# Attention with two feed-forward layers on one core: twenty conversion steps in the attention, fp32 centroid strips for every pair

## The chip, the cores and the metric

The kernel runs on one core of one Trainium2 chip. The metric is the time of one execution in device microseconds (us); lower is better. Of three executions shown for the kernel before, the median is 794.51 us (793.96 to 795.6).

## The reference

Clustered attention comes first, then two feed-forward layers. q, k and v have two batches, 8 heads, 768 rows and 64 columns; there are 16 centroids for each head. A row of q attends to the rows of k that have the same nearest centroid.

```python
q_assign = np.argmax(np.einsum('bhsd,hcd->bhsc', q_n, c_n), axis=-1)
k_assign = np.argmax(np.einsum('bhsd,hcd->bhsc', k_n, c_n), axis=-1)
mask = q_assign[:, :, :, None] == k_assign[:, :, None, :]
scores = np.where(mask, scale * q @ k.T, -1e9); attn = softmax(scores)
x = (attn @ v) reshaped to 1536 x 512
h = x @ w_in;  x = (h * cos(h)) @ w_out          # layer 0
h = x @ w_in2; x = g(h) @ w_out2                 # layer 1, g = a quadratic blend to a ReLU
```

All inputs are float32 except the four weight matrices (512 x 2048 and 2048 x 512), which come as float64.

## The kernel before

**Number format.** A large matmul takes each operand as a high and a low fp32r part (`hi`, the rounded value; `lo`, the rest). The scores use stacked tiles `st` that hold both parts, the layers use three matmuls for each product (`mm3`, L748 to L751).

**Weights.** The float64 weights come in 32 chunks of 1 MB (`wraw`, one buffer; `issue_chunk`, L130, on SP's queue). `convert_chunk` (L138) turns one chunk to fp32 with integer operations: Abs on ACT (L145), clamp, shift and two ORs on DVE (L147 to L155), hi on POOL (L161) with the issue of the next chunk behind it, lo on DVE (L164). The yields make six steps of it, and `pump(1)` does one step. In the attention, `run_slot` pumps at slots 69, 77, ... 189 (L686), 16 steps. In the layers, each of the four parts of `hidden` and `output` pumps one step; `weight` pumps what is missing. Two chunks make one weight tile: chunks 0 and 1 make `w_0`, which exists during the attention, chunks 2 and 3 make `w_1`, which exists only after it (L708).

**Attention.** A pair is two heads of one batch; there are eight. A pair has four units of six slots, so the attention has 192 slots. In a slot, `run_slot` (L664) emits for PE the transposes of the probabilities (L569), a score matmul pair for the unit ahead (L517, L520; eight slots ahead), and products with v (L594, L599, L600). DVE takes the row maximum (L526) and the low parts (L584), ACT the exponent (L535, in even slots) and the copies of the transposes (L572, L577, one in each slot). Slots before 18 and after 179 are ordered by readiness when the program is built; from 18 to 179 PE, ACT, DVE and POOL keep the order of the program (L694), SP does not.

**Preparation of a pair** (`prep_pair`, L294) runs a step in each slot, from slot -8 for pair 1 and 24(i-1)-16 for pair i. q and k are transposed (L349), copied from PSUM on ACT (L358), split to `th` and `tl`, and stacked by DMAs on SP's queue (L335; for pair 0 partly copied on POOL, L332). Then come the dot products with the centroids, and the argmax on DVE and POOL. Its one-hot rows are transposed (L434, L491) and written to `st`, for pair 0 by ACT and DVE (L446, L448), for the others by eight DMAs (L312) behind the next v load (L232), which waits until POOL has read the tile before it (L481, L482). PSUM gives three buffers for all of the transposes (`ps_t`).

- Pairs 0 and 1 (`NDVE`): DVE makes the low part (L316), and 24 matmuls of 64 columns (L408, L409) with the centroids as high and low part (`cn`) make the dots, which DVE then adds up (L377).
- Pairs 2 to 7: POOL splits (L321, L322), four fp32 matmuls of 32 rows each (strips, L389) with `cn32` make the dots, ACT copies them (L393), three transposes bring them back (L398).

**The start** has no other work for PE, so `run_idle` (L220) issues matmuls on zeros there; `NIDLE` gives their counts.

**The sums of a unit**: `inverse` (L541) adds the constant on POOL, five slots later DVE takes the reciprocal (L548), then POOL spreads it (L555).

Of the kernel before, what the change touches and what calls it, by code (L numbers as in the profile page):

```python
# [1 line left out]

# [6 lines left out]
F32 = mybir.dt.float32  # L9
# [9 lines left out]
P = 128  # L19
# [6 lines left out]
CHUNK = 6  # L26
P_BUFS = 6
NF = 2
NDVE = 2
NIDLE = (9, 3, 5, 7, 6)  # L30
# [3 lines left out]
def attention_moe_moe(  # L34
# [66 lines left out]
    cn = cpool.tile([P, NPAIR, 2, 2, C], F32R, name="cn")  # L101
# [36 lines left out]
    def convert_chunk(n):  # L138
# [4 lines left out]
        x = w0pool.tile([P, 2, 512], F32, tag="wx", bufs=1, name=f"wx{n}")  # L143
# [4 lines left out]
        yield  # L148
# [13 lines left out]
        issue_chunk(n + 1)  # L162
# [33 lines left out]
    with ExitStack() as actx:  # L196
# [44 lines left out]
        def centroid_setup(ct):  # L241
# [21 lines left out]
            nc.vector.memset(cn.bitcast(F32), 0.0)  # L263
# [3 lines left out]
        def centroid_parts(cd):  # L267
# [12 lines left out]
        def centroid_sum():  # L280

            for r in range(2):
                rows = slice(r * D, (r + 1) * D)
                nc.gpsimd.tensor_tensor(
                    cn32[rows, :, r], cn[rows, :, 0, r].bitcast(F32),
                    cn[rows, :, 1, r].bitcast(F32), ALU.add)
# [7 lines left out]
        def prep_pair(i):  # L294
# [19 lines left out]
            def qk_parts(s, cols, t32, pt, sc):  # L314
                if i < NDVE:
# [28 lines left out]
            for s in range(2):  # L344
                sc = D ** -0.5 if s == 0 else 1.0
                for hf in range(2):
# [6 lines left out]
                    if i < NDVE:  # L353
                        t32 = th[:, s, cols]
                    else:
                        t32 = ap.tile([P, HS], F32, tag="t32", bufs=4, name=f"t32_{i}_{s}_{hf}")
# [19 lines left out]
            def sum_dots(s, pd):  # L376
                nc.vector.tensor_reduce(  # L377
                    dotv[s].rearrange("p j h c -> p j (h c)"),
                    pd.rearrange("p j t h c -> p j (h c) t"), AX.X, ALU.add)

            rhs = cn[:, hp].rearrange("p t h c -> p (t h c)")
            pd32 = None
            if i >= NDVE:

                dt = ps_t.tile([P, HS], F32, tag="t", name=f"dt{i}")
                for hf in range(2):
                    for s in range(2):
                        g = (hf * 2 + s) * 2 * C
                        nc.tensor.matmul(  # L389
                            dt[g:g + 2 * C], cn32[:, hp].rearrange("p h c -> p (h c)"),  # L390
                            t32s[(s, hf)], start=True, stop=True, tile_position=(0, g))
# [9 lines left out]
            for s in range(2 if i < NDVE else 0):  # L401
                pd = ps_t.tile([P, NJ, 2, 2, C], F32, tag="t", name=f"pd{i}_{s}")
                for j in range(NJ):
                    cols = slice(j * P, (j + 1) * P)
                    o = pd[:, j if i == 0 else j % HJ * 2 + j // HJ].rearrange(
                        "p t h c -> p (t h c)")
                    with tc.issue_after(ins(tr)) if i == 0 else ExitStack():
                        nc.tensor.matmul(o, th[:, s, cols], rhs, start=True, stop=False)  # L408
# [430 lines left out]
```

## Time and profile before

| what | value |
|---|---|
| median of 3 executions | 794.51 us |
| the profiled execution, its own time | 794.65 us |
| its span, first to last instruction | 792.8 us |
| PE, DVE, ACT, POOL busy | 98%, 75%, 51%, 35% |
| mean granted clock of TensorE | 0.996 |

The span is the time between the first and the last instruction in the trace; 1.85 us of the execution lie outside it. PE's busy share says how long a matmul was under way. The granted clock is 1.00 at 2.4 GHz and 0.50 at 1.2 GHz.

### The profile page before, as it was taken

The page shows a single profiled execution, that of the slowest core. Times are in us where ns is not written, and L with a number is a line of the kernel's source. Part 1 is how long each engine was busy: PE and PEld are TensorE (multiplying, and loading weights), DVE is VectorE, ACT ScalarE, POOL GpSimd, SP SyncE. Part 2 cuts the span into 40 slices and gives each one's busy share as a digit, 9 for nine tenths or more (in the row PEclk, how much of TensorE's full clock was granted, in tenths as well). Part 3 has the DMA queues.
Part 4 walks back from the last instruction along what each step waited for, and adds up shares of the span by engine and source line. Part 5 has one row for each costly group of instructions (what it writes and reads, how often), then busy time and mean ns, then how long its engine had stood idle before and what let it go on. Part 6 is the DMA issues. An engine that isn't in the chain of part 4 may idle for free.

```text
span 792.8 us, 10973 instructions
## 1 busy us (share of the span) xinstructions
PE 779.4 (98%) x3963; PEld 635.9 (80%) x3964; DVE 596.7 (75%) x881; ACT 400.7 (51%) x768; POOL 275.8 (35%) x428
## 2 busy tenths in 40 slices
PE   8999999999999989999999999999999999999998
PEld 5777877878787868888888888888888888888886
DVE  6867877977989587778787878888878888655552
ACT  3788888888898555453334344322434323222220
POOL 4257567578545431221122212342131122111110
PEclk9999999999999999999999999999999999999999
DMA  7764754663420013222131121311121221000012
GB/s 167 172 153 113 176 130 105 144 175 94 106 79 29 26 53 107 79 81 107 54 98 62 58 101 54 107 54 53 58 103 54 90 71 53 1 1 0 22 46 93
DMA packets 48565, 65.94 MB, mean 83 GB/s; under 512 B 28032, under 2 KB 33024, under 8 KB 48512
## 3 DMA queue, kind: packets, MB, share of 16 engines
q1 hardware_dynamic: 48368, 65.22, 28.7%
q8 instruction: 31, 0.51, 0.3%
q14 instruction: 22, 0.18, 0.1%
q10 hardware_dynamic: 144, 0.03, 0.0%
HBM read 43.02 MB, written 3.15 MB: 58 GB/s over the span
## 4 chain that ended last, share of the span: by engine, by line
PE 88%; DVE 5%; ACT 4%; issue 1%; POOL 1%; SPq 1%; DMA 0%; ACTq 0%; POOLq 0%
PE y L751 11%; PE y L749 11%; PE y L750 11%; PE h L751 10%; PE h L749 10%; PE h L750 10%; PE pt L569 8%; PE s L517 4%; PE s L520 3%; PE o L594 2%; PE o L600 2%; PE o L599 2%; ACT p L535 1%; PE ptq L349 1%; DVE nm L526 1%
## 5 line engine op out<-in xcount | busy, mean ns | idle before, releaser
L711 POOL TENSOR_SCALAR gh<-g 128x512 fp32r<-128x512 f32 x96 | 70.9, 739 | 289.2 <-DVE g L742 163.8
L749 PE MATMUL h<-xh,w 128*128 128x512 f32 x384 | 149.5, 389 | 0.0
L751 PE MATMUL h<-xh,w 128*128 128x512 f32 x384 | 149.4, 389 | 0.0
L750 PE MATMUL h<-xl,w 128*128 128x512 f32 x384 | 149.4, 389 | 0.0
L526 DVE TENSOR_REDUCE nm<-s 128x1 f32<-128x768 f32 x96 | 91.4, 953 | 33.3 <-PE s L520 32.6
L569 PE MATMUL pt<-ident,p 128*128 128x128 f32 x576 | 98.2, 279 | 2.6 <-DVE plo L584 1.7
L738 ACT ACTIVATE p<-h,ones 128x512 f32<-128x512 f32 x48 | 33.0, 688 | 132.5 <-DVE m L737 132.1
L569 PEld LDWEIGHTS pt<-ident,p 128*128 128x128 f32 x576 | 68.3, 140 | 31.4 <-DVE nm L526 9.0
L535 ACT ACTIVATE p<-s,nm 128x768 f32<-128x768 f32 x96 | 86.4, 900 | 6.6 <-DVE nm L526 5.7
L715 DVE TENSOR_TENSOR gl<-g,gh 128x512 fp32r<-128x512 f32 x96 | 71.1, 741 | 20.8 <-POOL gh L711 15.0
L750 PEld LDWEIGHTS h<-xl,w 128*128 128x128 f32 x384 | 72.1, 188 | 15.0
L751 PEld LDWEIGHTS h<-xh,w 128*128 128x128 f32 x384 | 72.1, 188 | 15.0
L749 PEld LDWEIGHTS h<-xh,w 128*128 128x128 f32 x384 | 72.1, 188 | 14.9
L517 PE MATMUL s<-st,st 128*128 128x384 f32 x192 | 80.5, 419 | 1.5 <-ACT p L535 1.4
L145 ACT ACTIVATE wx<-wraw 128x1024 f32<-128x1024 f32 x32 | 36.4, 1138 | 88.0 <-DMA wraw<-in_moe_w_in_dram 32.7
L584 DVE TENSOR_TENSOR plo<-pt,phi 128x384 fp32r<-128x384 f32 x128 | 67.9, 549 | 14.1 <-ACT phi L577 13.8
L751 PE MATMUL y<-gh,w 128*128 128x512 f32 x192 | 75.6, 394 | 2.7 <-DVE w L164 2.7
L749 PE MATMUL y<-gh,w 128*128 128x512 f32 x192 | 75.3, 392 | 0.0
L750 PE MATMUL y<-gl,w 128*128 128x512 f32 x192 | 75.2, 392 | 0.0
L751 PE MATMUL y<-w,gl 128*128 128x512 f32 x192 | 74.7, 389 | 0.0
L749 PE MATMUL y<-w,gh 128*128 128x512 f32 x192 | 74.7, 389 | 0.0
L750 PE MATMUL y<-w,gh 128*128 128x512 f32 x192 | 74.7, 389 | 0.0
(132 smaller groups left out, 1530.0 us busy)
## 6 DMA issues: line engine op xcount, KB each, us to landing
wraw<-in_moe_w_in_dram SPq DMA_DIRECT2D x16, 1024.0 KB, 5.1
wraw<-in_moe_w_out_dram SPq DMA_DIRECT2D x16, 1024.0 KB, 4.7
st<-t SPq DMA_DIRECT2D x24, 192.0 KB, 4.2
st<-th SPq DMA_DIRECT2D x9, 384.0 KB, 4.0
st<-tl SPq DMA_DIRECT2D x18, 192.0 KB, 4.0
st<-th SPq DMA_DIRECT2D x18, 192.0 KB, 3.9
nat<-in_q_dram SPq DMA_DIRECT2D x8, 384.0 KB, 3.9
nat<-in_k_dram SPq DMA_DIRECT2D x8, 384.0 KB, 5.1
```

Of the source, the lines that this page charges most:

```text
L145: nc.scalar.activation(x, high.bitcast(F32), AF.Abs)
L517: nc.tensor.matmul(s[:, step, :HS], qt[:, 0, cols], kt[:, 0, kc], start=True, stop=False)
L526: nc.vector.tensor_reduce(nm, s[:, :, :HS], AX.XY, ALU.max, negate=True)
L535: nc.scalar.activation(p, s[:, :, :HS], AF.Exp, bias=nm, accum_out=dens[u][:, jj, 0:1])
L569: nc.tensor.transpose(ps[:, jj * P:(jj + 1) * P], p[:, kt * P:(kt + 1) * P], ident)
L584: nc.vector.tensor_tensor(lo, ps, hi.bitcast(F32), ALU.subtract)
L711: nc.gpsimd.tensor_scalar(hi, g, 1.0, 0.0, ALU.mult, ALU.add)
L715: nc.vector.tensor_tensor(lo, g, hi.bitcast(F32), ALU.subtract)
L738: nc.scalar.activation(r, ph, AF.Relu, bias=mone)
L749: nc.tensor.matmul(o, lh, rh, start=first, stop=False)
L750: nc.tensor.matmul(o, lh, rl, start=False, stop=False)
L751: nc.tensor.matmul(o, ll, rh, start=False, stop=last)
```

## The change

1. Conversion: 20 steps at slots 77, 83, 89, 95, 101, 105, 111, 115, ... 171, 175. Chunks 2 and 3 (`EARLY`) run interleaved: first all steps of both that give fp32 in `wx` (now two buffers), in four steps each with clamp and shift in one, and after the attention their hi and lo. The issue of the chunk after an early one follows its last OR.
2. Pairs 0 and 1 use `cn32` strips too. Pair 1 takes the way of pairs 2 to 7. Pair 0 keeps its low part on DVE, has an fp32 copy and a rounded copy on ACT, two strip matmuls and three transposes for q and for k each, and its maxima read PSUM. `cn`, its sums and `sum_dots` are gone.
3. Half of pair 0's one-hot rows of k are written by ACT.
4. For units 0 to 3 the constant and the reciprocal are on DVE, one behind the other.
5. Idle matmuls behind pair 0's two one-hot transposes: 5 and 3, not 7 and 6. `plo` has four buffers, not five.

```diff
+EARLY = (2, 3)
-NDVE = 2
-NIDLE = (9, 3, 5, 7, 6)
+NIDLE = (9, 3, 5, 5, 3)
...
-        x = w0pool.tile([P, 2, 512], F32, tag="wx", bufs=1, name=f"wx{n}")
+        x = w0pool.tile([P, 2, 512], F32, tag="wx", bufs=2, name=f"wx{n}")
...
         nc.vector.tensor_scalar(x, x, HIGH_MIN, HIGH_MAX, ALU.max, ALU.min)
-        yield
+        if n not in EARLY:
+            yield
...
+        if n in EARLY:
+            issue_chunk(n + 1)
+            yield
...
     def weight_steps():
-        for n in range(len(wchunks)):
-            for _ in convert_chunk(n):
-                yield n
+        n = 0
+        while n < len(wchunks):
+            if n != EARLY[0]:
+                yield from convert_chunk(n)
+                n += 1
+                continue
+            both = [convert_chunk(m) for m in EARLY]
+            for count in (4, 2):
+                for steps in both:
+                    yield from islice(steps, count)
+            n += len(EARLY)
...
-                nc.scalar.activation(cn[rows, :, 0, r], pcv[rows, :, r], AF.Copy)
-                nc.vector.tensor_tensor(
-                    cn[rows, :, 1, r], pcv[rows, :, r], cn[rows, :, 0, r].bitcast(F32),
-                    ALU.subtract)
-            later(6, centroid_sum)
+                nc.scalar.activation(cn32[rows, :, r], pcv[rows, :, r], AF.Copy)
...
-                if i < NDVE:
+                if i == 0:
                     nc.vector.scalar_tensor_tensor(
...
                     nc.scalar.activation(t32, pt, AF.Copy, scale=sc)
+                    if i == 0:
+                        nc.scalar.activation(th[:, s, cols], pt, AF.Copy, scale=sc)
...
+            if i == 0:
+                dcs = []
+                for s in range(2):
+                    dt = ps_t.tile([P, HS], F32, tag="t", name=f"dt0_{s}")
+                    for hf in range(2):
+                        g = hf * 2 * C
+                        with tc.issue_after(ins(tr)):
+                            nc.tensor.matmul(dt[g:g + 2 * C], cw, t32s[(s, hf)],
+                                             start=True, stop=True, tile_position=(0, g))
...
+                    if s == 0:
+                        nc.vector.tensor_copy(dc.rearrange("p j n -> p (j n)"), dt[:4 * C])
+                    else:
+                        nc.scalar.activation(dc.rearrange("p j n -> p (j n)"), dt[:4 * C], AF.Copy)
+                    dcs.append(dc)
+                for s in range(2):
+                    pd = ps_t.tile([P, HJ, 4 * C], F32, tag="t", name=f"pd0_{s}")
+                    for jj in range(HJ):
+                        mm = nc.tensor.transpose(pd[:, jj], dcs[s][:, jj], ident[:4 * C, :4 * C])
...
+                            elif par:
+                                nc.scalar.activation(
+                                    dst, src, AF.Identity, bias=own[r0:r0 + 2 * C, 1, h:h + 1],
+                                    scale=own[r0:r0 + 2 * C, 0, h:h + 1])
...
+            if u < 4:
+                nc.vector.tensor_scalar(den[:, :, 0], den[:, :, 0], 1e-9, 1.0, ALU.add, ALU.mult)
+                reciprocals(u, den)
+                return
...
-            lo = ap.tile([P, HS], F32R, tag="plo", bufs=5, name=f"plo{u}_{kt}")
+            lo = ap.tile([P, HS], F32R, tag="plo", bufs=4, name=f"plo{u}_{kt}")
...
+        CONVERT = (77, 83, 89, 95, *(n for n in range(101, 180) if n % 10 in (1, 5)))
...
-            if 64 <= slot < 192 and slot % 8 == 5:
+            if slot in CONVERT:
                 pump(1)
```

## Rows read from the trace of the kernel before

**Rows 1.** The page: busy us (share of the span) and instructions of each engine.
```profile
PE 779.4 (98%) x3963; PEld 635.9 (80%) x3964; DVE 596.7 (75%) x881; ACT 400.7 (51%) x768; POOL 275.8 (35%) x428
```

**Rows 2.** Busy us by stretch: PE, PEld, DVE, ACT, POOL; then granted clock, DMA share, GB/s.
```profile
20.00:40.00 20.00, 18.02 (x117) 14.79 (x116) 16.98 (x28) 14.26 (x32) 4.65 (x12) 1.00 0.76 176
100.00:250.00 150.00, 148.16 (x983) 119.85 (x979) 122.99 (x202) 127.93 (x288) 98.62 (x158) 1.00 0.45 110
```

**Rows 3.** PE's waits from 256 us on: us in total, times, longest.
```profile
PE y L751 <- DVE w L164: 2.7, 1, 2.7
```

**Rows 4.** The same view as rows 2: first output block, and a later one.
```profile
284.05:299.48 15.43, 12.72 (x50) 9.93 (x48) 12.73 (x17) 6.50 (x11) 5.42 (x6) 0.89 0.33 105
310.36:321.24 10.88, 10.88 (x50) 9.01 (x48) 8.99 (x11) 5.59 (x9) 2.34 (x4) 1.00 0.23 93
```

**Rows 5.** Timeline of the start: start, us, engine, line, operands, idle before.
```profile
5.67 0.87 ACT L358 ACTIVATE th<-ptq 128x384 fp32r<-128x384 f32 x2 [0.91 <-PE ptq L349]
...
11.00 0.35 DVE L426 TENSOR_REDUCE mx<-dots 128x12 f32<-128x192 f32 x1
...
12.16 0.54 DVE L377 TENSOR_REDUCE dots<-pd 128x192 f32<-128x384 f32 x1
...
14.57 0.36 DVE L430 TENSOR_TENSOR dots<-eq,mx 128x192 f32<-128x192 f32 x1
```

**Rows 6.** Timeline of PE and DVE from there to the first scores.
```profile
14.24 2.31 PE L224 MATMUL idle_o<-idle 128*128 128x512 bf16 x7
...
16.39 0.49 PE L434 MATMUL po<-ident,dots 128*64 128x128 f32 x3
...
16.92 2.74 DVE L448 TENSOR_SCALAR st<-po,own 32x384 fp32r<-32x384 f32 x4 [1.99 <-PE po L434]
...
18.42 0.41 PE L520 MATMUL s<-st,st 96*128 96x384 f32 x1
...
21.72 0.44 PE L517 MATMUL s<-st,st 128*128 128x384 f32 x1 [1.18 <-ACT p L535]
```

**Rows 7.** Timeline of PE: two dots of pair 1, the strips of pair 2.
```profile
23.33 0.28 PE L408 MATMUL pd<-cn,t 128*128 128x64 f32 x1
...
23.56 0.28 PE L408 MATMUL pd<-cn,t 128*128 128x64 f32 x1
...
46.04 0.85 PE L389 MATMUL dt<-t,cn 128*32 128x384 f32 x8
```

**Rows 8.** POOL's split of pairs 2 to 7: busy us, mean ns, idle before.
```profile
L322 POOL TENSOR_TENSOR tl<-t,th 128x384 fp32r<-128x384 f32 x16 | 16.4, 1027 | 1.3
...
L321 POOL TENSOR_SCALAR th<-t 128x384 fp32r<-128x384 f32 x16 | 8.2, 513 | 0.6 <-ACT t L358 0.6
```

**Rows 9.** Timeline of SP's queue from slot 101 on, then from slot 131 on.
```profile
160.55 0.37 SPq L232 DMA_DIRECT2D natv<-in_v_dram  x1
161.02 4.98 SPq L312 DMA_DIRECT2D st<-oht  x8
166.10 0.53 SPq L135 DMA_DIRECT2D wraw<-in_moe_w_in_dram  x1
...
202.44 0.48 SPq L335 DMA_DIRECT2D st<-tl  x1
```

**Rows 10.** Line 135 alone, 166 to 167 us: the transfer issued at 166.10.
```profile
DMA to landing us min/median/max: 5.5/5.5/5.5
```

**Rows 11.** Timeline of ACT from slot 111 to chunk 1's Abs.
```profile
167.79 0.51 ACT L577 ACTIVATE phi<-pt 128x384 fp32r<-128x384 f32 x1
...
169.03 0.90 ACT L535 ACTIVATE p<-s,nm 128x768 f32<-128x768 f32 x1
...
175.64 1.18 ACT L145 ACTIVATE wx<-wraw 128x1024 f32<-128x1024 f32 x1
```

**Rows 12.** Line 152, 100 to 256 us: duration in ns, min, median, max.
```profile
L152 DVE SCALAR_TENSOR_TENSOR wx<-wraw,wx x3: 1194/1457/1735, 145.1 to 251.0; 128x1024 int32<-128x1024 int32 x3
```

More of the change, by code (lines that the diff above doesn't have):

```diff
@@ L1 @@
 from contextlib import ExitStack
+from itertools import islice
 import concourse.bass as bass
@@ L100, in attention_moe_moe @@
     xl = cpool.tile([P, NPAIR, NT], F32R, name="xl")
-    cn = cpool.tile([P, NPAIR, 2, 2, C], F32R, name="cn")
     cn32 = cpool.tile([P, NPAIR, 2, C], F32, name="cn32")
@@ L161, in convert_chunk @@
         nc.gpsimd.tensor_scalar(hi, x, 1.0, 0.0, ALU.mult, ALU.add)
-        issue_chunk(n + 1)
+        if n not in EARLY:
+            issue_chunk(n + 1)
         yield
@@ L262, in centroid_setup @@
                 nc.vector.tensor_scalar(cd[:, r], ct[:, 0], ss[:, 3:4], None, ALU.mult)
-            nc.vector.memset(cn.bitcast(F32), 0.0)
             nc.gpsimd.memset(cn32, 0.0)
@@ L273, in centroid_parts @@
                 rows = slice(r * D, (r + 1) * D)
-                nc.scalar.activation(cn[rows, :, 0, r], pcv[rows, :, r], AF.Copy)
-                nc.vector.tensor_tensor(
-                    cn[rows, :, 1, r], pcv[rows, :, r], cn[rows, :, 0, r].bitcast(F32),
-                    ALU.subtract)
-            later(6, centroid_sum)
[L280 to L286, printed above, removed]
+                nc.scalar.activation(cn32[rows, :, r], pcv[rows, :, r], AF.Copy)
         prepped = {}
@@ L352, in prep_pair @@
                     cols = slice(hf * HS, (hf + 1) * HS)
[L353 to L356, printed above, removed]
+                    t32 = ap.tile([P, HS], F32, tag="t32", bufs=4, name=f"t32_{i}_{s}_{hf}")
                     t32s[(s, hf)] = t32
                     nc.scalar.activation(t32, pt, AF.Copy, scale=sc)
+                    if i == 0:
+                        nc.scalar.activation(th[:, s, cols], pt, AF.Copy, scale=sc)
                     later(1, qk_parts, s, cols, t32, pt, sc)
@@ L374, in prep_pair @@
                 for s in range(2)]
[L376 to L383, printed above, removed]
+            cw = cn32[:, hp].rearrange("p h c -> p (h c)")
+            pds = []
+            if i == 0:
[7 more added lines that the diff above has]
+                                             start=True, stop=True, tile_position=(0, g))
+                    dc = ap.tile([P, HJ, P], F32, tag=("oht", "xt2")[s], bufs=1 + s, name=f"dc0_{s}")
+                    dc = dc[:4 * C]
+                    if s == 0:
[7 more added lines that the diff above has]
+                        mm = nc.tensor.transpose(pd[:, jj], dcs[s][:, jj], ident[:4 * C, :4 * C])
+                    pds.append(pd.rearrange("p jj (f h c) -> p (jj f) h c", h=2, c=C))
+                yield
+            else:
                 dt = ps_t.tile([P, HS], F32, tag="t", name=f"dt{i}")
@@ L388, in prep_pair @@
                         g = (hf * 2 + s) * 2 * C
-                        nc.tensor.matmul(
-                            dt[g:g + 2 * C], cn32[:, hp].rearrange("p h c -> p (h c)"),
-                            t32s[(s, hf)], start=True, stop=True, tile_position=(0, g))
+                        nc.tensor.matmul(dt[g:g + 2 * C], cw, t32s[(s, hf)],
+                                         start=True, stop=True, tile_position=(0, g))
                 dc = ap.tile([P, HJ, P], F32, tag="eq", bufs=1, name=f"dc{i}")
@@ L400, in prep_pair @@
                 yield
[L401 to L408, printed above, removed]
-                    mm = nc.tensor.matmul(o, tl[:, s, cols], rhs, start=False, stop=True)
-                    if j % 3 == 2:
-                        if j == NJ - 1:
-                            later(1, sum_dots, s, pd)
-                        yield
             G = NJ * 4
@@ L420, in prep_pair @@
                 for s in range(2):
-                    dv = dotv[s]
+                    dv, dp = dotv[s], pds[s]
                     m = mx[:, s * G // 2:(s + 1) * G // 2].rearrange("p (j h) -> p j h", h=2)
@@ L425, in prep_pair @@
                     db = desc.unsqueeze(1).unsqueeze(1).to_broadcast([P, NJ, 2, C])
-                    nc.vector.tensor_reduce(m, dv, AX.X, ALU.max)
-                    nc.vector.tensor_tensor(e, dv, mb, ALU.is_ge)
+                    nc.vector.tensor_reduce(m, dp, AX.X, ALU.max)
+                    nc.vector.tensor_tensor(e, dp, mb, ALU.is_ge)
                     nc.vector.tensor_tensor(e, e, db, ALU.mult)
@@ L442, in prep_pair @@
                             dst = st[h][s][D:D + 2 * C, 1].rearrange(
-                                "c (jp par n) -> c jp par n", par=2, n=P)[:, :, par]
+                                "c (par jp n) -> c par jp n", par=2, n=P)[:, par]
                             src = po[r0:r0 + 2 * C]
@@ L453, in prep_pair @@
                 mb = mx.unsqueeze(2).to_broadcast([P, G, C])
-                dp = dv if pd32 is None else pd32.rearrange("p j (g c) -> p (j g) c", c=C)
+                dp = pd32.rearrange("p j (g c) -> p (j g) c", c=C)
                 yield
```

## The prediction

> **What bounds the kernel now.** I first read the busy shares. PE is under way 98% of the span [rows 1], so only two things save time: less PE work, or less PE idleness. The table by stretch says where the idleness is. From 100 to 250 us PE idles 150.00 - 148.16 = 1.84 us in all, from 20 to 40 us 1.98 us [rows 2]. PE's waits after 256 us have one large row: 2.7 us for DVE's last part of a weight tile [rows 3]. In the stretch of the first output block, 48 matmuls take 15.43 us and the granted clock averages 0.89; a later block of 48 takes 10.88 us at 1.00 [rows 4]. The wait and the half clock behind it thus cost 15.43 - 10.88 = 4.55 us, of which 2.7 is the wait and 1.8 the clock at its lower level. From 310 us on nothing is to be had.
>
> The sum is made against the profiled execution, 794.65 us: its span of 792.8 and 1.85 around it. That is 0.14 above the median of 794.51. A difference of 0.2%, 1.6 us, is about what a measurement of this kernel can tell from none.
>
> **First term, the end of the attention: -4.55.** Before, the sixteen steps end inside chunk 2; the rest of it and all of chunk 3 come between the layers' first matmuls, and PE waits for chunk 3's lo. With twenty steps both early chunks are fp32 before the layers begin, and four pumps, one in each part of the first hidden block, write hi, lo, hi, lo. That is some 11 us before the output block asks for them. DVE is 12.73 of 15.43 us busy in the block [rows 4], and has fewer steps there than before. What is late next is the low part of the hidden values; the wait list has no row for it [rows 3], so I count the whole 4.55. If those parts came in late after all, the 1.8 of the clock would still go.
>
> **Second, pair 1's dots: -1.4.** Two small matmuls take 0.23 us, 23.33 to 23.56 [rows 7], so 24 take 12 x 0.23 = 2.8 us. The strips take 0.85 us [rows 7], the three transposes, at the 0.16 that a transpose of three in 0.49 takes, at 16.39 [rows 6], 0.5: 1.35 in all. PE has this work between scores and is busy there, so 1.4 us goes from the path. The Trainium skill (TensorEngine Tiling (Array Packing), Key Properties) says that a switch of the tiling mode drains TensorE, which speaks against strips. [...]
>
> **Third, the start: -2.0.** This chain has many links. (a) ACT has two copies for each part, not one; two take 0.87 [rows 5], so each extra one costs 0.43. A part's PSUM buffer is free only when the low part is made behind the second copy, and there are three buffers: k's second transposes come some 0.8 us later, the low part of k 0.9 later. (b) The strips and the three transposes of each half then give the first maximum at about 10.8, against 11.00 [rows 5], since the adding up of the dots is gone. (c) From there to the last compare DVE needs 14.57 + 0.36 - 11.00 = 3.9 us, 0.54 of it the other half's adding up [rows 5]; without it 3.4, so 14.2. (d) Before, k's one-hot transposes wait behind 7 idle matmuls of 0.33 each and start near 16.2 [rows 6]. With five behind a transpose that ends near 13.3 they start at 13.3 + 1.65 = 14.95: 1.2 us earlier. (e) DVE's four writes take 2.74, 0.68 each, and the first full score needs two of them [rows 6]. Now ACT does the second beside the first: 0.7 less. (d) and (e) make 1.9, with (b) 2.0, and the score at 18.42 comes at 16.4. Bounds: nothing, if the order on ACT costs what DVE saves; 3.0, if PE keeps its full clock there and (d) costs only 5 x 0.23, which is what a matmul of 512 columns takes in 10.88 / 48 [rows 4].
>
> **Fourth, 20 to 40 us: -0.6.** Of the 1.98 us idle, 1.18 is the wait for the first exponent, before 21.72 [rows 6], which stays. DVE, 16.98 of 20 us busy [rows 2], loses two of the four writes, pair 1's low parts and the adding up of its dots; I take 0.6 of the remaining 0.8. POOL takes the split instead: four times 0.51 + 1.03 = 6.2 us [rows 8] where it is 4.65 of 20 us busy [rows 2]. That is hidden; if POOL were late, pair 1's stacking DMAs would be, by the 1.5 us of one part, and its scores, which begin only in slot 16, would take a part of that. The constant on DVE for four units adds four small operations and takes a hop away that PE does not wait for: nothing. Four `plo` buffers: at most three are alive at once, nothing.
>
> **Fifth, four more steps in the attention: +0.8.** Sixteen steps and all else leave PE 1.84 us idle [rows 2], 0.12 a step, so four cost 0.5. Clamp and shift now stand back to back on DVE, once beside a maximum of pair 7: 0.3 more. Bounds: 0.2 and 2.0. The OR takes from 1194 to 1735 ns [rows 12]. The Trainium skill (SBUF — State Buffer, Who interferes with whom) says that a DVE instruction with two SBUF inputs and a GpSimd one that reads SBUF block each other. The trace agrees as far as this spread goes; by it the two more ORs of an early chunk would cost 0.5 each where POOL is reading, and the term 1.8.
>
> **Sixth, a new wait on ACT: +3.3.** Chunk 1's transfer can be issued once chunk 0's last OR is done, in slot 101, before as after. But SP's queue holds, in that slot, the next v load, which waits for POOL until 160.55, and eight one-hot copies of 4.98 us; the chunk goes out at 166.10 [rows 9] and lands 5.5 us later [rows 10], at 171.6. Before, Abs of chunk 1 stands in slot 117 on ACT, at 175.64. Now it stands in slot 111, whose ACT copy ends at 167.79 + 0.51 = 168.3 [rows 11]. ACT keeps the program's order there, so it would stand still from 168.3 to 171.6, 3.3 us. Queued behind it are the copy of slot 112 and its exponent, at 169.03 [rows 11], the last of three that the transposes of slot 114 need. Even without a wait it would end at 169.03 + 1.18 + 0.90 = 171.1, just in time, so I give PE no slack and count the 3.3 in full. All of this moves earlier together with the start, so the difference stays. Bounds: 0, if the chunk goes out ahead of the copies, and 3.3 + 1.8, if PE's clock falls behind it as it does in rows 4. Chunk 2's Abs is in slot 141: at (175.64 - 167.79) / 6 = 1.3 us a slot it comes 30 slots on, near 206, and its transfer, if issued behind the copies of slot 125 and ahead of pair 7's stacking, lands near 202. Chunk 3 is issued in slot 155 and read in slot 161, six slots of 1.3 against 5.5 and the OR's 1.2: at most a few tenths, left in the range.
>
> **Sum.** -4.55 - 1.4 - 2.0 - 0.6 + 0.8 + 3.3 = -4.45: 794.65 - 4.45 = 790.2.
>
> **The rivals.**
>
> *A, the forecast*, 790.2 (788.6 to 791.4 with the bounds of the start and the steps): chance 0.40.
>
> *B, no wait for chunk 1.* SP is not held to the program's order, so the chunk may go out before the copies, or POOL may be done earlier. For it: the OR ends well before 160. Against it: before, with the same OR in the same slot, it went out after them [rows 9]. 790.2 - 3.3 = 786.9: chance 0.20.
>
> *C, the start gains nothing.* Three PSUM buffers serve eleven tiles of pair 0, and ACT has four more copies; the readiness order may put the rounded copies ahead. For it: step (a). Against: the seven idle matmuls alone hold PE until 16.2. 790.2 + 2.0 = 792.2: chance 0.17.
>
> *E, the wait of term six halves the clock.* For it: the only other idleness of 2.7 us did [rows 4]. Against: PE's idleness may fall apart into shorter ones. The Trainium skill (TensorE: Matmul & The Clock Gate, HAM oscillation — how this bites in real kernels) says that waits between bursts of matmuls throttle the clock again, so by that page E would be the likelier; the trace has one such case. 790.2 + 1.8 = 792.0: chance 0.10.
>
> *D, slower: every early chunk arrives late.* Place: ACT in slots 111, 141 and 161. If chunk 2's transfer goes out behind pair 7's five stacking DMAs, it is issued after 202.44 + 0.48 and lands at 208.4 [rows 9, 10], 2.4 us after its Abs is due; chunk 3 adds 0.5. With the clock down behind each of the three, 790.2 + 2.4 + 0.5 + 3 x 1.8 = 798.5. It decides once more than 4.45 + 1.6 is added to A. For it: ACT is 128 of 150 us busy [rows 2] and cannot catch up much. Against: those DMAs wait for a tile that is free only near 198 us, later than the OR. Chance 0.13.
>
> **How the numbers follow.** The time is A's, 790.2. Leaving out D and the lowest of B, 785.8 to 793.8 holds 8 in 10: from B with a start better by 1.0 to C with 1.6 of E's clock. Faster by over 0.2% means below 792.9: A and B, most of E (0.09) and half of C (0.08), 0.77. Within: the rest of C and E, 0.10. Slower: D, 0.13.
>
> **What the profile after would show.** First term: no wait of the output block for L164's successor, and a block of 10.9 us. Second and third: strips at the start, the first full score at 16.4 or so, no 64-column matmuls. Sixth: on ACT an idle time of about 3 us before the second Abs, released by the raw chunk's DMA, and PE idle by the same in 165 to 175 us. I am wrong if that idle time is missing (B), if the first score stays near 18.4 (C), or if the clock is at 0.50 anywhere between the start and the layers (E, D).

## The result, and the profile after

The changed kernel takes 799.86 us (median of four executions, 799.73 to 800.09); the kernel before, run beside it, 794.24. The ratio is 1.007, with an interval of 1.0055 to 1.0085: the change costs 5.6 us, where 4.3 fewer were predicted. The profiled execution took 799.8 us with a span of 798.0, 5.2 above the span before. The half clock of [rows 4] is not in every execution of the kernel before: of the 101 that stand beside the experiments below, twelve have a mean granted clock of 1.000 and take 793.14 to 794.32 us.

The page's busy shares of the changed kernel:

```profile
PE 780.2 (98%) x3936; PEld 630.6 (79%) x3936; DVE 595.5 (75%) x873; ACT 404.0 (51%) x776; POOL 280.8 (35%) x430
```

PE's 98% answers to [rows 1] and hides the loss: 5.2 us are 0.7% of the span. The table by stretch has it (the stretches of [rows 2], then the first output block and a later one as in [rows 4]):

```profile
20.00:40.00 20.00, 18.82 (x105) 12.75 (x104) 13.72 (x24) 13.18 (x32) 12.06 (x20) 1.00 0.80 179
100.00:250.00 150.00, 143.80 (x943) 115.01 (x942) 121.57 (x198) 123.57 (x278) 97.80 (x151) 1.00 0.48 117
...
290.69:301.57 10.88, 10.88 (x49) 9.01 (x48) 10.19 (x15) 6.28 (x11) 4.37 (x5) 1.00 0.28 96
316.80:327.68 10.88, 10.88 (x50) 9.01 (x49) 8.73 (x11) 5.81 (x10) 2.34 (x4) 1.00 0.23 90
```

The first output block now takes 10.88 us at full clock, exactly as forecast. From 100 to 250 us PE idles 150.00 - 143.80 = 6.2 us instead of 1.84. With the forecast's steps (0.8) and its wait on ACT (3.3) it would be 5.9, but most of the 6.2 lies in other waits than those. PE's waits from 100 to 256 us, the whole list:

```profile
PE pt L579 <- DVE plo L594: 4.3, 8, 1.1
PE ptq L350 <- DVE plo L594: 1.0, 1, 1.0
PE s L523 <- ACT p L541: 0.7, 1, 0.7
PE pt L579 <- ACT p L541: 0.2, 1, 0.2
```

Before, the same list had 1.0 in two waits for `plo`:

```profile
PE pt L569 <- DVE plo L584: 1.0, 2, 0.6
```

Now it is 5.3 in nine: DVE makes the low part of the probabilities late, nine times, never by more than 1.1 us.

To see where time goes I follow the slots by ACT's copies of the transposed probabilities, one in each slot: the copy of slot n after less that before. The layers I follow by the first matmul of each block.

| place | after less before, us |
|---|---|
| slot 8 / 12 / 24 / 68 | -1.5 / -0.5 / -0.5 / -0.5 |
| slot 96 / 104 / 112 / 120 | -0.9 / +0.3 / +4.1 / +2.6 |
| slot 136 / 148 / 160 / 184 | +2.6 / +4.4 / +4.9 / +5.7 |
| first hidden block / first output block / the block behind it | +5.6 / +6.6 / +2.1 |
| just ahead of the border of the layers / behind it | +2.1 / +5.2 |

So there are four accounts: the start gains 1.5 and gives 1 back at once; the attention loses 6; the first hidden blocks lose 1.1 and the first output block returns 4.55; the border of the layers, of which the prediction has no word, takes 3.1.

**The start.** PE, changed kernel: one-hot transposes, first full score, then pair 1's strips.

```profile
13.33 0.49 PE L436 MATMUL po<-ident,dots 128*64 128x128 f32 x3 [0.79 <-DVE dots L432]
...
14.73 0.49 PE L436 MATMUL po<-ident,dots 128*64 128x128 f32 x3
...
16.08 0.41 PE L526 MATMUL s<-st,st 96*128 96x384 f32 x1
...
21.85 0.83 PE L405 MATMUL dt<-t,cn 128*32 128x384 f32 x2
...
22.99 0.84 PE L405 MATMUL dt<-t,cn 128*32 128x384 f32 x4
...
24.23 0.83 PE L405 MATMUL dt<-t,cn 128*32 128x384 f32 x2
```

The score comes at 16.08 instead of 18.42 [rows 6]. But pair 1's strips are three groups of 0.83, not one of 0.85 [rows 7]. Timeline of POOL, SP's queue and PE behind it:

```profile
21.72 1.95 POOL L323 TENSOR_TENSOR t<-t,t 128x384 fp32r<-128x384 f32 x2
...
24.37 1.42 POOL L488 TENSOR_TENSOR vv<-natv,vv 128x256 fp32r<-128x256 f32 x2
...
25.82 0.37 SPq L246 DMA_DIRECT2D natv<-in_v_dram  x1
26.23 7.11 SPq L336 DMA_DIRECT2D st<-t  x9
33.39 0.94 SPq L227 DMA_DIRECT2D nat<-in_q_dram  x1
...
39.17 0.55 PE L350 MATMUL ptq<-ident,nat 128*128 128x128 f32 x3 [0.70 <-DMA nat<-in_q_dram]
```

SP's queue before:

```profile
21.54 0.53 SPq L232 DMA_DIRECT2D natv<-in_v_dram  x1
...
34.17 0.89 SPq L213 DMA_DIRECT2D nat<-in_q_dram  x1
```

POOL now splits pair 1 ahead of v's second part, so the next v load goes out at 25.82, not 21.54. Behind it stand the stacking transfers (`st<-t`), which wait for that split, and behind these pair 2's q rows. The rows go out only 0.8 us sooner than before, where the slots ahead of them are 1.5 sooner, and PE waits 0.70 us for them.

**Slots 105 to 112.** POOL, DVE, PE, SP's queue and ACT:

```profile
160.70 1.04 POOL L165 TENSOR_SCALAR w<-wx 128x1024 fp32r<-128x1024 f32 x1
...
161.77 1.51 DVE L169 TENSOR_TENSOR w<-wx,w 128x1024 fp32r<-128x1024 f32 x1 [1.17 <-POOL w L165]
...
163.81 0.55 PE L350 MATMUL ptq<-ident,nat 128*128 128x128 f32 x3 [0.98 <-DVE plo L594]
...
166.31 0.53 SPq L135 DMA_DIRECT2D wraw<-in_moe_w_in_dram  x1
...
171.52 1.12 ACT L145 ACTIVATE wx<-wraw 128x1024 f32<-128x1024 f32 x1 [1.68 <-DMA wraw<-in_moe_w_in_dram]
...
173.67 0.62 PE L579 MATMUL pt<-ident,p 128*128 128x128 f32 x3 [1.13 <-DVE plo L594]
```

Chunk 0's lo stands four slots behind its hi, in slot 105, where before it was eight. DVE keeps the program's order, so it stands still 1.17 us for POOL with the low parts queued behind it. Then ACT waits for chunk 1, as forecast, but 1.68 us, not 3.3, since it is late by then.

**Behind it** each stall is small. Two of the last three steps (slots 165 and 171), DVE, then PE:

```profile
238.60 0.69 DVE L147 TENSOR_SCALAR wx<-wx 128x1024 f32<-128x1024 f32 x1
239.32 0.88 DVE L150 TENSOR_SCALAR wx<-wx 128x1024 int32<-128x1024 int32 x1
240.12 1.00 DVE L594 TENSOR_TENSOR plo<-pt,phi 128x384 fp32r<-128x384 f32 x2
...
246.08 1.83 DVE L153 SCALAR_TENSOR_TENSOR wx<-wraw,wx 128x1024 int32<-128x1024 int32 x1
247.83 1.01 DVE L594 TENSOR_TENSOR plo<-pt,phi 128x384 fp32r<-128x384 f32 x2
```
```profile
240.81 0.52 PE L579 MATMUL pt<-ident,p 128*128 128x128 f32 x3 [0.46 <-DVE plo L594]
...
248.52 0.52 PE L579 MATMUL pt<-ident,p 128*128 128x128 f32 x3 [0.69 <-DVE plo L594]
```

A step of 1.57 us (clamp and shift together) or 1.83 (an OR) stands ahead of two low parts, and PE's next transposes wait for the first of these.

**The layers.** First hidden block, then the border (DVE, POOL, PE):

```profile
275.03 3.08 DVE L169 TENSOR_TENSOR w<-wx,w 128x1024 fp32r<-128x1024 f32 x2
...
279.36 0.50 PE L760 MATMUL h<-xh,w 128*128 128x512 f32 x1 [0.43 <-DVE g L739]
...
556.74 2.50 POOL L165 TENSOR_SCALAR w<-wx 128x1024 fp32r<-128x1024 f32 x2
...
558.25 2.06 DVE L169 TENSOR_TENSOR w<-wx,w 128x1024 fp32r<-128x1024 f32 x1
...
560.83 1.21 DVE L169 TENSOR_TENSOR w<-wx,w 128x1024 fp32r<-128x1024 f32 x1
...
560.96 0.50 PE L760 MATMUL y<-w,gh 128*128 128x512 f32 x1 [0.83 <-DVE acc L799]
...
564.77 0.47 PE L760 MATMUL h<-xh,w 128*128 128x512 f32 x1 [0.79 <-ACT p L749]
```

PE's waits after 256 us, the whole list, to set against [rows 3]:

```profile
PE h L760 <- ACT p L749: 1.0, 2, 0.8
PE y L760 <- DVE acc L799: 0.8, 1, 0.8
PE h L760 <- DVE g L739: 0.4, 1, 0.4
```

The wait of 2.7 for a weight's low part is gone, as forecast; three kinds of shorter ones are new. At the border two hi stand back to back on POOL and two lo on DVE within 4 us, with the last sums (`acc`) of layer 0 between them. Before, the two lo there were 11 us apart:

```profile
551.42 1.21 DVE L164 TENSOR_TENSOR w<-wx,w 128x1024 fp32r<-128x1024 f32 x1
...
562.42 1.62 DVE L164 TENSOR_TENSOR w<-wx,w 128x1024 fp32r<-128x1024 f32 x1 [0.35 <-POOL w L161]
```

### The profile page after: what moved, and what is told of

The parts are those of the page before. It is cut to its first block, busy times and chain, and to the rows that moved or that the text cites. A ratio compares the mean times of both kernels' runs of the same rounds, so it can differ in the third digit from the quotient of the medians.

```text
span 798.0 us, 10930 instructions
## 1 busy us (share of the span) xinstructions
PE 780.2 (98%) x3936; PEld 630.6 (79%) x3936; DVE 595.5 (75%) x873; ACT 404.0 (51%) x776; POOL 280.8 (35%) x430
## 4 chain that ended last, share of the span: by engine, by line
PE 53%; DVE 26%; POOL 6%; DMA 6%; ACT 5%; issue 4%; SPq 0%; POOLq 0%; ACTq 0%; DVEq 0%
PE pt L579 7%; PE y L760 5%; PE y L762 5%; PE y L761 5%; PE h L760 4%; PE h L762 4%; PE h L761 4%; DVE gl L726 4%; POOL gh L722 4%; PE s L523 3%; PE s L526 3%; DVE g L739 3%; DMA wraw<-in_moe_w_out_dram 3%; DVE wx L153 3%; DVE w L169 3%
## 5 line engine op out<-in xcount | busy, mean ns | idle before, releaser
L722 POOL TENSOR_SCALAR gh<-g 128x512 fp32r<-128x512 f32 x96 | 68.2, 711 | 322.7 <-DVE g L753 185.2
L726 DVE TENSOR_TENSOR gl<-g,gh 128x512 fp32r<-128x512 f32 x96 | 74.1, 773 | 20.3 <-POOL gh L722 13.4
```

Of the source, the lines that this page charges most:

```text
L722: nc.gpsimd.tensor_scalar(hi, g, 1.0, 0.0, ALU.mult, ALU.add)
L726: nc.vector.tensor_tensor(lo, g, hi.bitcast(F32), ALU.subtract)
```

## The experiments

In all of them the ratio is that to the kernel before, run beside it; "border" is what is lost across the border of the layers.

**e1: the change without its conversion**, and **e2: the conversion alone** (in the kernel before, with four `plo` buffers).

```diff
 # e1
-EARLY = (2, 3)
+EARLY = (-1, -1)
-        ... tag="wx", bufs=2
+        ... tag="wx", bufs=1
-            if slot in CONVERT:
+            if 64 <= slot < 192 and slot % 8 == 5:
```

> The changed kernel with the conversion of the kernel before (16 steps at slots 69, 77, ... 189, chunks 2 and 3 not interleaved, one wx buffer). Theory (the conversion steps make the loss; the strips and the start are worth little, since pair 1's strips come in three groups and the next pair's load is late): 793.3 to 794.2, the first full score near 16.1 and slot 24 only 0.5 us earlier than before. Rival (the POOL split of pair 1 makes the loss): above 796. Second rival (the start's 2.3 us come through where the conversion does not spoil it): 791.5 to 792.5.

> The kernel before with the new conversion alone (20 steps at the new slots, chunks 2 and 3 interleaved, two wx buffers, four plo buffers). Theory (the conversion makes the loss by itself): 799.5 to 801, with slot 184 some 6 us later than before, the first output block without its wait, and 3 us lost again at the border of the two layers. Rival (it loses only beside the strips, whose POOL work delays it): 790 to 793.

e1: 794.34 against 794.36 (0.9997, 0.9986 to 1.0009). The first score is as in the changed kernel, slot 8 is 1.4 early, slots 12 to 92 only 0.4. e2: 801.56 (1.0085, 1.0068 to 1.0102): slot 112 +3.3, slot 184 +5.2, border +5.2. So the loss is the conversion's, and the rest of the change, alone, is worth nothing as it stands.

**e3: one fp32 buffer for every late chunk** (in the changed kernel).

```diff
-        x = w0pool.tile([P, 2, 512], F32, tag="wx", bufs=2, ...)
+        x = w0pool.tile([P, 2, 512], F32, tag="wx3" if n == EARLY[1] else "wx", bufs=1, ...)
```

> The changed kernel with one wx buffer for every chunk but chunk 3, which has a buffer of its own. Theory (at the border of the layers two chunks wait with both their hi and lo for the same weight tile, and DVE does both lo ahead of the accumulation): the border's 3.1 us go, 796.5 to 797.0. Rival (the steps are four places earlier in the layers, and that phase makes the stall): 799.5 to 800.

799.21 (1.0056, 1.0035 to 1.0076). The border falls from 3.1 to 1.3, less than expected. The first hidden block is at +6.0, where the changed kernel has +5.6, so the time hardly moves.

**e7: the step counter's phase.** The other reason for the border was that 20 steps, not 16, shift all later steps by four.

```diff
-            pump(1)
+            if (l, qi, blk) != (0, 0, 1):
+                pump(1)
```

> The changed kernel, but the second hidden block pumps no conversion step, so that from the third block on every chunk has the place it had before; the two wx buffers stay. Theory (the place of the steps in the layers makes the stall at their border): it goes, 796.3 to 797.0. Rival (two wx buffers alone make it): 799.3 to 800.

801.79 (1.0092, 1.0079 to 1.0106), border 5.3: the phase theory fell. Over all runs, the border took 3.1 to 6.0 in the seven kernels with two (the changed one, e2, e4, e6, e7, e12, e14) and 0.4 to 1.4 in the six with four early chunks and one buffer for the late ones (e3, e8, e11, e13, e15, e16). So it is the second buffer; e3 changes nothing else. How is read from the traces: it lets the fp32 steps of a chunk run ahead of the chunk before, and the two hi and lo bunch up (in e3 the two lo are 11 us apart again, at 557.25 and 568.24). What puts the border at 3.1 in one kernel and at 6.0 in another stays open.

**e4: a second buffer for `natv`**, so that a v load on SP's queue, ahead of pair 2's rows and later of chunk 1, waits for POOL no longer, and **e6: chunk 0's lo and chunk 1's Abs later.**

```diff
 # e6
-        CONVERT = (77, 83, 89, 95, 101, 105, 111, 115, 121, 125, ...
+        CONVERT = (77, 83, 89, 95, 101, 109, 117, 119, 121, 125, ...
```

> The changed kernel with two buffers for the v tile that POOL splits, so that the next v load on SP's queue waits no longer for POOL. Theory (SP's queue held by that load makes pair 2's rows late at 38 us and chunk 1's raw words late at 171 us): slot 16 about 2 us earlier than before, not 0.5, chunk 1 lands before its Abs is due, 796.0 to 797.5. Rival (the transfers themselves are the limit there): 799 to 800 and landings at the same times.

> The changed kernel with chunk 0's lo in slot 109 (not 105) and chunk 1's Abs and clamp in slots 117 and 119 (not 111 and 115). Theory (lo in 105 holds DVE until POOL has the hi, and Abs in 111 holds ACT until the raw words land): slot 120 some 2.5 to 3.5 us earlier than in the changed kernel, and the same gain at slot 184. What the layers add (3.1 us in the changed kernel, 5.2 in e2) is not foretold: 796 to 799.5 in all. Rival (the steps' own work on DVE makes the loss): slot 120 less than 1 us earlier.

e4: 799.79 (1.0057, 1.004 to 1.0074). Chunk 1 lands at 166.9, ahead of its Abs at 169.3; slot 120 is at +0.8 instead of +2.6, but slot 184 still at +3.9. At the start the theory fell: slot 16 is 0.9 early, not 2. SP's queue in e4:

```profile
16.70 0.47 SPq L246 DMA_DIRECT2D natv<-in_v_dram  x1
21.80 11.56 SPq L336 DMA_DIRECT2D st<-t  x10
33.40 0.92 SPq L227 DMA_DIRECT2D nat<-in_q_dram  x1
```

The v load goes out at 16.70, and pair 2's q rows no sooner than in the changed kernel (33.39): what holds them is the ten stacking transfers, and these wait for POOL's split of pair 1 (7.0 us of SP's waits from 14 to 40 us).

e6: 800.22 (1.0069, 1.0055 to 1.0083). Slot 120 is at +0.1: the wait for POOL and that for the chunk were the 2.5 us there, and no more. Slot 184 is at +4.0 all the same: slots 120 to 184 lose another 4 by themselves. (Its border took 6.0, so the time did not fall.) So the expected gain held at slot 120 and not at slot 184.

**e5: pair 2's rows ahead** (e1 with one line moved), for the wait at 39.17.

```diff
             load_v(1)
+            load_qk(2)
...
-            elif i < len(pairs) - 1:
+            elif 1 < i < len(pairs) - 1:
```

> The kernel of e1 (strips, conversion as before) with the load of pair 2's q and k moved from behind pair 1's ten stacking transfers to behind the first two v loads. Theory (the start's 2.3 us are lost at slot 8, where PE waits for pair 2's rows, because SP's queue is held by the v load that waits for POOL): no such wait, slot 16 earlier than before by 1.5 to 2.3 us, 792.2 to 793.2. Rival (another wait ends at the same place, a limit of the transfers or of ACT): 794.0 to 794.6 as e1.

792.96 against 794.28 (0.9987, 0.9978 to 0.9995). Slots 24 to 92 are 1.4 early instead of 0.4: the rows' place on the queue, behind the stacking transfers, held 1.0. (In the profiled execution, 794.28, the first output block gives 1.4 back: the granted clock is 0.50 from 286.4 to 293.2 us there, where before it was from 288.6 to 292.0.)

**e8: all of that together**: e5's rows, chunk issue right behind the last OR, steps spread over slots 69 to 169, one buffer for late chunks.

> The changed kernel with all of it mended: pair 2's rows early as in e5; each of the first four chunks' next transfer issued right behind its last OR, the steps spread over slots 69 to 169 with no lo sooner than eight slots behind its hi; one wx buffer for the layers and a second one for chunks 1 and 3; the four late steps spread over two hidden blocks, so that later chunks have the place they had before. Theory (the losses are waits of the new step places, and the gain at the first output block is real): the first output block without its wait (-4.5 us), the start -1.5 to -2, no stall at the border, steps +0.5: 787.5 to 789.5. Rival (the attention loses what four steps more cost, wherever they stand): 791 to 793.

795.02 (1.0005, 0.9997 to 1.0014). The layers did as expected (first hidden block +1.05, output block -4.55, border 0.4), but the attention lost 5 again, 3.1 in slots 76 to 96 and 3.5 in slots 120 to 148, with none between. ACT's one wait for a chunk was 0.46 us, and DVE waited for no hi of POOL: neither was the cause.

**e9: the work that is left, between the layers' first blocks**: 17 steps in the attention, chunk 3 converted in the hidden blocks; and **e10: e5's sixteen steps six slots apart.**

> e5 with one more step in the attention (17, the last one chunk 2's second OR with chunk 3's issue behind it), an own fp32 buffer for chunk 3, and the eight steps that are left of chunks 2 and 3 in the first five layer parts (two, two, two, one, one). Theory (the first output block's 4.55 us can be had without twenty steps in the attention, whose price is the attention's slack): the attention ends within 0.5 of e5's, the first hidden block is up to 1.1 longer, the first output block takes 10.9 with no half clock behind it, the layer border stays: 794.3 - 1.5 - 4.5 + 0.5 = 788 to 789.5. Rival (the work that leaves the attention costs as much wherever it stands): the hidden blocks stall by 3 us or more, 791.5 to 793. A second rival: the seventeenth step alone costs the attention 2 or more, 790.5 to 791.5.

> e5 with its sixteen steps six slots apart (69 to 159), not eight. Theory (the attention has no slack on DVE and ACT for steps closer than about eight slots, whatever chunk they belong to): slots 120 to 160 come 1.5 to 3 us later than in e5 and only a part of it is recovered by 184, 793.5 to 795.5. Rival (only a wait for a raw chunk, or DVE behind POOL's hi, costs anything): as e5 by slot 184, within 0.7 of it, 792.5 to 793.5.

803.83 (1.0118, 1.01 to 1.0136) and 813.46 (1.0236, 1.0207 to 1.0266), both worse than either theory has it, for a reason in neither. POOL and DVE in e9:

```profile
161.16 1.04 POOL L165 TENSOR_SCALAR w<-wx 128x1024 fp32r<-128x1024 f32 x1 [13.21 <-DMA st<-oht]
```
```profile
166.63 0.55 DVE L644 TENSOR_TENSOR xt<-xt,r 128x384 f32<-128x384 f32 x1 [9.79 <-POOL xt L633]
```

`w_0` shares its memory with the split rows of pairs 1, 3 and 5 (tag `w_0`, line 301). Chunk 0's hi, put into slot 97 in e9 and 93 in e10, must wait until the DMAs of pair 5 have read these, near 160 us, and POOL, held to its order, stands for 13 us with DVE and PE behind it. So hi cannot stand much ahead of slot 101, where the kernel has it. Density was not tested by e10. Of e9 one thing remains: its two first hidden blocks lost 7 us more, so eight steps placed like that cost more than the 4.55 that they free.

**e11: more room.** Chunk 0 is issued in slot 38, the fp32 steps of chunks 0 and 1 stand in slots 51 to 97, hi in 103; otherwise e8.

> e8 with the steps spread wider: chunk 0 is issued in slot 38, not 60, the fp32 steps of chunks 0 and 1 stand in slots 51 to 97, where DVE in e5 is about 75% busy (60 to 110 us), chunk 0's hi in slot 103, and behind slot 101 there are as many DVE steps as before (one in about eight slots). Theory (DVE has no room for more than about a step in eight slots in the second half of the attention, and that was e8's loss): the attention ends 1 to 1.7 earlier than in the kernel before, the first hidden block is 1.1 longer, the first output block takes 10.9: 789 to 790.5. Rival (four more steps and two lo cost 4 to 5 wherever they stand): slots 60 to 100 already lose 2 or more, 793 to 795.

794.17 (0.9991, 0.9982 to 1.0). The attention still lost 4.7 against e5, 2.7 of it by slot 100. The steps did not all stand where I thought: from 60 to 110 us DVE is 76% busy in e11, and there it lost 0.5, but slots 51 to 100 reach from 90 to 153 us, and from 90 to 157 DVE is 83% busy. Wider spacing alone brought little.

**e12: DVE's work taken away**: e6 without chunk 3's clamp, shift and ORs.

> e6 with chunk 3's clamp, shift and two ORs on DVE left out (about 4.3 us of DVE; Abs, the transfers, hi and lo stay; so layer 0's first output weight is not the right one). Theory (the loss of slots 120 to 184 in e6, from +0.1 to +4.0, is DVE's time): slot 184 comes at +0.5 to +1.5 against the kernel before, the rest as in e6, 796.5 to 798. Rival (it is ACT's Abs or the transfers beside the stacking DMAs): slot 184 at +3 or more, 799.5 to 800.5.

798.17 (1.004, 1.0029 to 1.005). Up to slot 160 as e6 (+3.0); then slot 184 at +1.7 where e6 is at +4.0. So it is chunk 3's instructions on DVE that cost these 2.3 us, not its Abs and not the transfer, which stayed. 1.7 lies just above my expectation, which had forgotten that chunks 1 and 2 keep theirs.

**e13: the same steps, other slots.** A pair has 24 slots. The kernel before has its steps at slots 5, 13 and 21 of these, since 69 + 8k comes to no other. The changed kernel and e11 have them at odd slots all over. e13 differs from e11 only in its slots: every DVE step stands at 5, 9, 13 or 21, Abs and hi between them (but for the last Abs, at 5).

```diff
-  ((51, 55, 59, 65, 69, 103, 111), (77, 81, 87, 91, 97, 109, 119), (117, 123, 131, 137, 145), (155, 159, 165, 173, 179))
+  ((51, 53, 57, 61, 69, 103, 109), (75, 77, 81, 85, 93, 107, 117), (115, 125, 129, 133, 141), (149, 153, 157, 165, 173))
```

> e11 with the same steps in other slots: every DVE step stands in slot 5, 9, 13 or 21 of a pair's 24 (the old steps stood in 5, 13 and 21), where the trace of e5 shows DVE's other work short; Abs and hi stand elsewhere. Nothing else differs. Theory (what the twenty steps cost in the attention is where in a pair's 24 slots a DVE step stands: in slots 17 to 3 it meets the argmax of the next pair and makes the low part of the probabilities late): the attention ends 0.5 to 1.7 earlier than in the kernel before, against 3.0 later in e11, and the layers keep e11's -3.2: 789 to 791. Rival (DVE's time as such, or ACT's: the number of steps decides): within 1 us of e11, 793.2 to 795.

790.84 against 793.92 (0.9959, 0.9945 to 0.9972). Slot 184 is at -1.0, where e11 has +3.0.

**e14: the changed kernel with another list**, nothing else.

```diff
-        CONVERT = (77, 83, 89, 95, *(n for n in range(101, 180) if n % 10 in (1, 5)))
+        CONVERT = (75, 77, 81, 85, 101, 109, 115, 117, 125, 129, 133, 141, 145, 149, 153, 157, 163, 165, 173, 177)
```

> The changed kernel with nothing but its slot list changed: the same twenty steps in the same order, every DVE step in slot 5, 9, 13 or 21 of a pair's 24, Abs one to six slots ahead of it, chunk 0's hi still in slot 101 and its lo in 109. Theory (the change's loss in the attention is the place of its steps, with the two hidden blocks' 1.1 and the layer border's 3.1 unchanged and the first output block 4.55 shorter): slot 184 at -0.5 to +1.5 against the kernel before, not +5.7; 793.8 to 796.5. Rival (e13 was good for its earlier start and its single buffers, not for the places): slot 184 at +3 or more, 797.5 to 800.

796.43 against 794.14 (1.0018, 1.0008 to 1.0029). Slot 184 goes from +5.7 to -0.8; 2.5 of that are the waits at slots 105 to 120, which this list avoids as e6 does. The table by stretch and PE's waits from 100 to 256 us of e14:

```profile
100.00:250.00 150.00, 147.99 (x981) 120.07 (x980) 127.06 (x205) 128.28 (x288) 102.61 (x155) 1.00 0.47 117
```
```profile
PE pt L579 <- DVE plo L594: 1.4, 4, 0.4
PE s L523 <- ACT p L541: 0.5, 1, 0.5
```

DVE is busy 127.06 us of 150, against 121.57 in the changed kernel, and yet PE idles 2.0 us instead of 6.2. DVE had the time; what differs is where the steps stand. What is left above before in e14 is the border, 5.7 us here.

**e15 and e16: pair 1's strips in one group** (in e13). e15 asks that they be issued behind the last copy on ACT, e16 issues the last strip first and the other three behind it on PE's own queue.

```diff
 # e16
-                for hf in range(2):
-                    for s in range(2):
+                for hf in (1, 0):
+                    for s in (1, 0):
+                        with tc.issue_after(ins(tail)) if i == 1 and tail is not None else ExitStack():
```

> e13 with pair 1's four strips held back until the last copy of its rows is done, so that they can go out in one group. Theory (a group of strips takes 0.83 us whatever it holds, and pair 1's three groups make 2.5 us where one makes 0.85): PE has 1.6 us less to do near 22 us; slots 0 to 16 come 0.5 to 1.6 earlier than in e13, 789.2 to 790.3. Rival (PE waits there for the exponent or DVE anyhow): slots 16 and on within 0.3 of e13, 790.5 to 791.2.

> e13 with pair 1's strips in another order: the one whose rows are copied last is issued first and the other three behind it, so that they make one or at most two groups (e15's edit had left three groups as they were). Theory (a group takes 0.83 us whatever it holds, and each group less gives PE 0.8 us there): slots 16 and on come 0.8 to 1.6 earlier than in e13, 789.2 to 790.1. Rival (the time comes back as idleness: PE waits there for an exponent, DVE or the maxima that come later): slots 16 and on within 0.4 of e13, 790.5 to 791.3.

e15 left the three groups as they were (791.27; 0.9961, 0.9949 to 0.9973) and tells nothing. e16: 789.44 against 794.25 (0.9935, 0.9922 to 0.9947). PE in e16:

```profile
23.08 0.85 PE L398 MATMUL dt<-t,cn 128*32 128x384 f32 x8
```

One group of 0.85, and slot 24 comes at -3.6 instead of -1.4. That is 2.2 us, more than the 1.65 of two groups; 0.3 of the rest stands already at the first full score (15.79 against 16.08 in e13), ahead of the strips. e16 beats both kernels, by 4.8 and 10.4 us.

## Why the prediction was wrong, term by term

No single term did it. By the profiled executions the sum was 9.7 us too low (-4.45 against 5.2), and the places of the table share it out: the start was to give 4.0 and has 0.5 left at slot 68 (3.5 off); the steps were to cost 0.8 and the wait on ACT 3.3, and the attention loses 6.2 from slot 68 to 184, of which 0.2 come back behind it (1.9 off); the first hidden blocks take 1.1 that was not counted; the border takes 3.1 that was not counted.

**First, -4.55: right**, and to the hundredth: the block takes 10.88. But the four pumps that pay for it were costed at nothing ("has fewer steps there than before"). Two lo back to back on DVE, 3.08 us, cost 1.1 in the hidden blocks. PE's wait at 279.36 is not for the low part of the hidden values, which the text named as "late next", but for the product `g` (L739), which reads the hidden values from PSUM and stands on DVE behind the two lo.

**Second, -1.4: the size was wrong.** I took 0.85 from a row with all four strips in one group; where order goes by readiness they went out as their rows came, three times 0.83 = 2.5 us, with the three transposes 3.0, against 2.8: the term came to nothing. A group costs the same with one strip in it (two instructions), two or four. e16 gives the term back in full. The Trainium skill (TensorEngine Tiling (Array Packing), Key Properties) says that a change of tiling mode drains TensorE. In the trace of before little of it shows outside a group: the two matmuls ahead of the strips start 0.18 us apart (45.60 and 45.78), the strips 0.26 behind the second (46.04). Whether a drain is a part of the 0.83 these rows don't tell, since it too would come once for each group.

**Third, -2.0: right for the score** (16.08, forecast 16.4), but only to slot 8. The 0.3 beyond the forecast are its own bound: five idle matmuls took 1.24 us, not 1.65, since the granted clock is 1.00 there, where it was 0.72 from 14.24 to 16.55 before. (The bound of 3.0 does not follow from the text: 5 x 0.1 more is 2.5. The lowest of B with 1.0 off is 785.9, not 785.8.) The step that failed is in the fourth: "That is hidden; if POOL were late, pair 1's stacking DMAs would be". They were held by POOL, but I followed them only to pair 1's scores. Behind them on SP's queue stand pair 2's rows, and these came too late for the earlier slots: 1.0 us (e5), which freeing the v load does not give back (e4). I had moved work to POOL without asking what stands on the queue behind the transfers that wait for it. e5 and e16 together have slot 24 at -3.6, close to the -4.0 of the three terms: the gains were there, behind two small things.

**Fifth, +0.8 (0.2 to 2.0): sized far too small.** I divided 1.84 us of idleness by sixteen steps and took the 0.12 as a price for any step. That price was read from steps at slots 5, 13 and 21 of a pair alone. With its list the change loses 6.2 from slot 68 to 184 (-0.5 to +5.7), of which 2.5 are the two waits at slots 105 to 120 (e6) and the rest elsewhere; with e14's list it loses nothing. The Trainium skill (SBUF — State Buffer, Who interferes with whom) says that a DVE instruction with two SBUF inputs contends with a GpSimd one that reads SBUF; the border shows such a spread (a lo of 1.21 us took 2.06 beside POOL's hi), but the estimate made from it, 1.8, was also short.

e12 shows for chunk 3 that DVE's instructions make the loss, e13 and e14 that the list of slots does (Abs moved along with the DVE steps). Step by step the traces agree. I take what is lost from the slot ahead of a DVE step to the fifth behind it, in the changed kernel, e6, e8, e11, e13 and e14. At places 5 and 13 (the slot's number in its pair's 24) that is never over 0.2 us, in 26 steps; at place 3 it is 0.7 to 1.4 in all four, at place 15 0.5 to 1.2 in six of eight. What exactly a step meets there is only argued: in e5's trace the argmax of the next pair has its DVE instructions in slots 18, 20, 0 and 2, but the stalls at 240.81 and 248.52 show no argmax beside them, and the first of them stands behind a step at place 21. Nor is the period shown: 5, 9, 13 and 21 are all one more than a multiple of four, and no run tells a period of 24 slots from a shorter one.

**Sixth, +3.3: the mechanism right, the size not**: 1.68 us on ACT, 1.13 on PE. It is not added to the fifth: e4 and e6 take the wait away and gain 1.8 and 2.5 at slot 120. That the fifth and the sixth together, 4.1, come as near to the 6.2 as they do is luck: one was far too small and the other too large.

**Left out: the border, +3.1.** The step that failed is that I costed the second `wx` buffer at nothing, without a sentence on it. It serves the early chunks and stays for the 28 late ones.

**The rivals.** B fell (the wait is there), C fell by its sign (the score is early), though by slot 24 its "gains nothing" is nearly what is left of the start; E and D's clock fell: the granted clock is 1.00 from 100 to 250 us. D came nearest in time, 798.5, by the wrong way: chunk 2 landed 3.3 us ahead of its Abs, and chunk 3's Abs started as it landed. The rivals looked at transfers, the start and the clock; none at the place of a step on DVE.

## What to carry to other kernels

In a hand-ordered pipeline the price of a step is a price of its place: take it only from steps that stand at the same place in the period, and when a list of slots changes, reduce it by the period first. An engine 80% busy has room, but not everywhere; here the same twenty steps cost 6 us, 2.5 of them in two waits, or nothing. And look up every buffer whose count or lifetime changes in all the places that use it later, and for an engine that gets more work every transfer that waits for it, with all that stands behind that transfer on the queue.

## What the runs showed of the hardware

- Strips of 32 columns in fp32 take 0.83 us in a group of two instructions, 0.84 in one of four and 0.85 in one of eight.
- In the changed kernel the granted clock stayed at 1.00 from 100 to 250 us through PE waits of up to 1.13 us and 6.2 us of idleness. It fell to one half in the block of [rows 4], at the end of a wait of 2.7, and in e9 and e10 in the stall behind POOL (PE waits of 6.5 and 10.8). But in the kernel before it was at one half from 12.1 to 15.5 us too, where PE's longest wait ahead of it was 1.05, at 8.87, and PE was busy 1.93 of the 2 us up to 12.0. So the length of the last wait alone does not say when it falls.
- POOL's hi of 1.04 us took 2.50 for two, and DVE's lo 2.06 instead of 1.21, where they stood beside each other at the border.
